# Weight loads on ScalarE's queue and set ask times in a planned DeltaNet and MLP kernel

## The chip, the cores and the metric

The kernel runs on one core of a Trainium2 chip. The metric is the device time of one execution in microseconds (us), as the median of several runs. Five engines work side by side on a core, each through its own instructions in order: TensorE (PE, matmuls), VectorE (DVE), ScalarE (ACT), GpSimd (POOL) and SyncE (SP, which here only issues DMA transfers). ACT and POOL can issue DMA transfers too. An engine that meets an instruction whose inputs are not ready stops there, and all that stands behind it waits.

## The reference

A delta-rule attention (4 batches, 8 heads, 768 tokens, head size 48), whose output goes through layer normalization and a two-layer MLP with a residual:

```python
for t in range(S):
    y[:, :, t] = np.einsum('bhd,bhde->bhe', q[:, :, t], state)
    v_old = np.einsum('bhde,bhd->bhe', state, kt)
    state = state + bt[:, :, :, None] * np.einsum('bhd,bhe->bhde', kt, vt - v_old)
...
xn = (x - mu) / np.sqrt(var + 1e-06) * g_ln
ch = np.maximum(xn @ w_ch1, 0.0) @ w_ch2
return (x + ch).astype(np.float32)
```

`kt` is the key divided by its norm. `x` is `y` with the heads side by side, 384 wide; `w_ch1` is 384 x 1536 and `w_ch2` 1536 x 384. All data is fp32.

## The kernel before

**Tiling.** The tokens are cut into 12 chunks of 64 (`C`), and a chunk is computed for all 32 sequences at once. Within a chunk the recurrence is solved in closed form: a triangular 64 x 64 system built from the products of keys (`gram`, tile `gsb`), whose inverse is `xt`. Chunk 0 gets its inverse by repeated matmuls (`first_inverse`, lines L853 to L910: products on PE, masks and transposes on DVE, copies into `xt` on ACT). Chunks 1, then 2 and 3, then 4 and 5 and so on get it by rows (`rows_inverse`): `gsb` is stored to DRAM (`gd`), loaded again with a sequence per partition (`gb`), ACT takes the norm (L1006), DVE works off one row after the other (L1025 and L1030), the result `xb` goes to DRAM (`xd`) and comes back as `xt`. `blocks_join` and `join` (PE at L1057, L1062, L1089, L1094) put the blocks of `xt` together. `recur` then makes u, the outputs y, the new state and the normalized `xnt` of the chunk, and `mlp` does the two products: the first at L1331 with a relu on ACT at L1340 into `h_all`; the second at L1353 for chunk 0, and for all others at L1429 in seven block products instead of eight. The first product of chunk 0 goes through two PSUM banks in turn.

**Weights.** They come in 12 pieces of 768 KB (`fetch`): six of `w_ch1`, then six of `w_ch2`, read as 32-bit words into five buffers. Pieces 0 and 1 go into `h_all`, the others in turn into three `words` buffers, so a piece from the sixth on can only be fetched when an earlier one is converted. Each is converted (`convert`) with two passes on ACT (L710, L718), one on DVE (L715) and one on POOL (L728), which writes `w_sb`.

**Other loads.** `load_raw` brings raw keys in four transfers of 96 KB (into `kr`, for chunk 3 into `tb`), `load_blocks` brings keys or queries in blocks of 32 tokens in eight small transfers (keys through POOL's queue, queries through SP's), `load_v` the values, and `norms` loads the diagonal of `gd` (`ksum`) with which the values are scaled. Almost all of it is issued by SP; ACT issues two loads of raw keys at the start.

**What sets the order.** The kernel does not issue as it goes. Every step is entered with `add` into a `Line`: its engine, an assumed cost, what it reads and writes, a priority (`pr`), for MLP products a due time (`due`), and an earliest time (`t0`). `Line.run` plays the whole kernel through on assumed times (`dma_go` moves the loads along, `LANES` = 8 loads on the way at most) and picks for each engine what comes next; `emit` issues the steps by planned start. `in_this_order` then ties each engine's instructions to that order. So `t0` and `due` are no waits on the chip: they move instructions within an engine's order. Where the plan leaves PE idle for long, `warm_up` puts in filler matmuls that compute nothing (L1507).

On the chip an instruction waits for semaphores. DMA transfers from SP and ACT share eight of them, and one that is issued waits until the eighth before it has landed.

Of the kernel before, what the change touches and what calls it, by code (L numbers as in the profile page):

```python
# [16 lines left out]
C = 64  # L17
# [6 lines left out]
@contextmanager  # L24
def in_this_order(tc):
    first = len(tc.nc.cur_bb.bb.instructions)
    last = {}
    yield last
    for ins in tc.nc.cur_bb.bb.instructions[first:]:
        if ins.engine not in ORDERED:  # L30
            continue
        if ins.engine in last:
            tc.add_manual_dep(
                ins, last[ins.engine].name,
                mybir.DependencyInfo(mybir.DependencyClass.NoSync, mybir.DependencyReason.DATA),
                reason="in_this_order",
            )
        last[ins.engine] = ins


PLAN = None
# [24 lines left out]
class Line:  # L66
# [6 lines left out]
    PE_TAIL, SWITCH = 0.12, 0.1  # L73
    BLOCK, FIRST, FETCH = 128, 93, 3.95
    WINDOW, WARM, KEEP = 3.413, 0.44, 0.6
    DMA_ISSUE, DMA_DONE, LANES = 1.35, 0.65, 8

    def __init__(self):
        self.steps = []
# [86 lines left out]
    def dma_go(self, until):  # L166

        while self.dma_t < until - 1e-12:
            on = [q for q in self.rings.values() if q and q[0][2] <= self.dma_t + 1e-12]
            lim = min([until] + [q[0][2] for q in self.rings.values() if q and q[0][2] > self.dma_t + 1e-12])  # L170
            if not on:
                self.dma_t = lim
                continue
            dt = min(lim - self.dma_t, len(on) * min(q[0][1] for q in on))
            for q in on:
                q[0][1] -= dt / len(on)
            self.dma_t += dt
            landed = False
            for q in on:
                if q[0][1] <= 1e-9:  # L180
                    s = q.pop(0)[0]
                    s.end = self.dma_t + self.DMA_DONE
                    self.done(s)
                    landed = True
            if landed:
                return True
        return False

    def dma_next(self):
        on = [q for q in self.rings.values() if q and q[0][2] <= self.dma_t + 1e-12]  # L190
        t = [q[0][2] for q in self.rings.values() if q and q[0][2] > self.dma_t + 1e-12]
        if on:
            t.append(self.dma_t + len(on) * min(q[0][1] for q in on))
        return min(t) if t else None

    def done(self, s):
# [191 lines left out]
def kernel(  # L388
# [28 lines left out]
    GH = 2 * H  # L417
# [11 lines left out]
    def sb(name, shape, dt=FP32):  # L429
# [12 lines left out]
    WORD_KEYS = [[("words", i)] for i in range(3)] + [  # L442
        [("h", 6 * i + f, g) for f in range(6) for g in range(2)] for i in range(2)
    ]
    tb = [sb(f"tb{i}", [128, GH * 64]) for i in range(3)]
    NKT, NQT, NPT, NG, NX, NV = 4, 2, 2, 4, 4, 2
# [31 lines left out]
    beta_b = sb("beta_b", [128, NSL, BK])  # L478
# [5 lines left out]
    ksum = [sb(f"ksum{i}", [128, GH]) for i in range(2)]  # L484
# [30 lines left out]
    def half(e):  # L515
        return slice(C * e, C * e + C)
# [15 lines left out]
    def dma(eng, out_, in_, n, ns, r=(), w=(), **kw):  # L532

        cost = 0.65 if eng != "SP" else 0.45 if n <= 512 else 0.62
        add(eng, cost, lambda: QUEUE[eng].dma_start(out=out_, in_=in_), r, w, bulk=n * ns / 16e3, **kw)  # L535
# [41 lines left out]
    for n in MASKED:  # L577
        k_, m, w = min(n, 4) if n == 6 else n, masks[n] if n < 6 else mask4, C if n < 6 else BK
# [52 lines left out]
    def load_padded(i, src, c, engs, **kw):  # L631
        for e in range(2):
            dma(
                engs[e], tb[i].rearrange("p (h d) -> p h d", d=DP)[half(e), :, 0:D], nat(src, c, e),
                GH * C, 16.5, [], [("tb", i, e, g) for g in range(2)], **kw,
            )

    def load_v(c, **kw):
        for e in range(2):
            dma("SP", vs[c % NV][half(e)], nat(v, c, e), GH * C, 16.5, w=[("v", c % NV, e)], **kw)  # L640

    def load_raw(c, engs=("SP", "SP"), dst=None, keys=None, **kw):

        dst = kraws[c % 3] if dst is None else dst
        for hp in range(2):
            for e in range(2):
                o = e ^ hp
                dma(
                    engs[e], dst.rearrange("p (h d) -> p h d", d=DP)[half(o), hp::2, 0:D],
                    k[2 * e : 2 * e + 2, hp::2, c * C : (c + 1) * C, :].rearrange("g h p d -> p (g h) d"),  # L650
                    NP * 2 * C, 16.5, [], [("kr", c % 3, o, hp)] if keys is None else [keys[2 * hp + e]], **kw,
                )

    def load_blocks(i, src, c, eng, **kw):
        dst = tb[i].rearrange("p (h u d) -> p h u d", u=2, d=BK)
        for hp in range(2):
            for m in range(2):
                w = min(BK, D - BK * m)
                p0 = DP * hp + BK * m
                for u in range(2):  # L660
                    t0 = c * C + BK * u
                    dma(
                        eng, dst[p0 : p0 + BK, :, u, 0:w],
                        src[:, hp::2, t0 : t0 + BK, BK * m : BK * m + w].rearrange("b j t d -> t (b j) d"),
                        GH * BK, 13.7 if w == BK else 11, [("tbpad", i)], [("tb", i, hp, m, u)],
                        after=[("tb", i, e, g, *o) for e in range(2) for g in range(2) for o in ((), (1,))], **kw,
                    )
# [25 lines left out]
    def fetch(i, **kw):  # L693
        dst = words[BUF[i]].rearrange("p n w -> p (n w)")
        src = pieces[i][1]
        if len(src.shape) == 3:
            dst = dst.rearrange("p (t n) -> p t n", t=2)
        dma("SP", dst, src, 256, 115, w=WORD_KEYS[BUF[i]], **kw)

    def convert(i, c0=0, n=WN, **kw):  # L700

# [410 lines left out]
    def norms(c, **kw):  # L1112
        i = c % 2
        flat = gpads[c % NG].rearrange("p h t -> (p h t)")
        w = GH * C
        for e in range(2):
            own = flat[e * C * w : e * C * w + C * (w + 1)].rearrange("(s x) -> s x", x=w + 1)[:, 0:w:C]
            dma("SP", ksum[i][half(e)], own, GH * C, 11, [("gd", c % NG)], [("ks", i, e)], **kw)
        kk = [("kn", i, n) for n in range(2)]
        add("ACT", 0.22, lambda: nc.scalar.sqrt(knrm[i], ksum[i]), [("ks", i, e) for e in range(2)], kk, **kw)  # L1120
        add("Pool", 0.2, lambda: nc.gpsimd.tensor_scalar_add(knrm[i], knrm[i], 1e-6), [], kk + [("kn", i)], **kw)
        scale_v(c, knrm[i], kk, **kw)
# [193 lines left out]
        return fbanks[turns[0] % 2] if not turns[1] else fbanks[turns[1] % 3]  # L1316

    def due(c, t):
        return 42.0 + 40.2 * c + 1.35 * t * (1.0 if c else 1.6) - (22.0 if c > 1 else 3.0 if c else 0.0)

    def mlp(c):
        xnt, x = xnts[c % 2], xs[c % 3]
# [176 lines left out]
        dma("Pool", brow[BK * e : BK * e + GH], beta[2 * e : 2 * e + 2, :, 0:C].rearrange("g h t -> (g h) t"), GH, 20, w=[("brow", e)], **chain)  # L1499
    load_v(0, pr=-79)  # L1500
    for i in range(3):
        fetch(i, pr=-70 + i)
    for i in range(3, 5):
        fetch(i, pr=-60 + i)

    def zeros():
        nc.tensor.matmul(f_[0][:, 256:512], nought, nought[:, 0:1].to_broadcast([128, 256]))  # L1507
# [26 lines left out]
    def prep_g(m):  # L1534
        pr = 20 * m - 15
        for c in (2 * m, 2 * m + 1):
            kt = (kts[c % NKT], ("kt", c % NKT))
            if c == 2:
                load_raw(c, pr=pr, t0=12.0)
                first_kt(kraws[2], raw_keys(2), *kt, PAIRS[3], pr=pr, t0=40.0)  # L1540
            elif c == 3:
                keys = [("tb", 2, e, hp) for hp in range(2) for e in range(2)]
                load_raw(c, dst=tb[2], keys=keys, pr=pr, t0=12.0)
                first_kt(tb[2], keys + [("tbpad", 2)], *kt, PAIRS[3], pr=pr, t0=40.0)
            else:
                load_blocks(2 * (c % 2), k, c, "Pool", pr=pr, t0=40.0 * m - 50)
                turned(c, 2 * (c % 2), *kt, pr=pr)
            gram(c, PAIRS[3 if m == 1 else 0], pr=pr, lag=0.5)

# [11 lines left out]
    for n, (p0, c, rows, cols) in enumerate(spots(BK, (0, 1))):  # L1561
        e, t0 = rows.start // C, c * C + cols.start
        dma(
            "SP", beta_b[p0 : p0 + GH],
            beta[2 * e : 2 * e + 2].rearrange("g h (m s) -> (g h) m s", m=NSL)[:, :, t0 : t0 + BK],
            96, 13.7, w=[("beta_b", n)], pr=5, t0=30.0,
        )

    def prep_x(m):
# [4 lines left out]

    def step(c):
        pr = 10 * c
        t0 = {2: 72.0, 3: 95.0}.get(c, 0.7)
        load_v(c, pr=pr - 5, t0=t0)
        if c > 2:
            load_raw(c, pr=pr - 5, t0=t0)  # L1580
        norms(c, pr=pr - 2)
        load_blocks(1, q, c, "SP", pr=pr - 3, t0=t0)
        turned(c, 1, qts[c % NQT], ("qt", c % NQT), pr=pr - 2)
        queries(c, pr=pr - 1, lag=0.5)
        recur(c, pr, lag=0.8)

    load_padded(1, q, 1, ("SP", "SP"), pr=8.2, t0=20.0)
    load_v(1, pr=8.1, t0=20.0)
    norms(1, pr=4)
    blocks_join(1, pr=3)  # L1590
    join(1, pr=3)
# [56 lines left out]
```

## Time and profile before

| what | value |
|---|---|
| median of 3 runs | 572.99 us (571.78 to 575.56) |
| profiled execution, its own time | 575.68 us |
| profiled execution, span from first to last instruction | 573.7 us |
| mean granted clock of TensorE | 0.964 |
| busy, PE / weight loads / DVE / ACT / POOL | 533.7 / 468.0 / 323.4 / 173.0 / 229.2 us |
| first MLP matmul of chunk 0 / of chunk 1 | 63.5 / 127.6 us |
| first product of the MLP, L1331 | 864 records, 209.8 us busy, 389 ns each |
| second product of chunks 1 to 11, L1429 | 924 records in three groups, 98.6 + 92.4 + 32.3 us busy |
| ten weight pieces into `words` | 768 KB each, median 10.0 us from issue to landing |
| two weight pieces into `h_all` | 768 KB each, median 6.4 us from issue to landing |
| moved by all DMA | 54.56 MB, 95 GB/s in the mean |

Times in the trace count from the start of the span. A matmul of the program is two records in the trace. Busy matmuls overlap, so busy time is more than what they cost one after the other. "SPq" is SP's queue of DMA issues, "ACTq" ACT's; a time beside them is that of issuing, not of the transfer. What stands in brackets with an arrow at a row of the timeline is the idle time of the engine before it, and what ended it. Idle time of an engine matters only where something waits for that engine.

### The profile page before, as it was taken

What the parts mean: (1) busy time and instruction counts of PE and PEld (TensorE: products, weight loads), DVE (VectorE), ACT (ScalarE), POOL (GpSimd) and SP (SyncE); (2) the same over time, 40 slices, a digit from 0 to 9 for tenths busy, and PEclk for the clock granted to TensorE, in tenths of its full rate; (3) what the DMA queues carried; (4) which work ended last, traced back from release to release, by engine and by line L of the source; (5) the groups of instructions that cost most, each with busy time, mean ns of one, the idle gap of its engine ahead of it and who ended that gap; (6) DMA issues with size and microseconds to landing.
All of it is one profiled execution on the core that took longest, in us unless ns stands there. A gap on an engine that the chain in (4) does not pass through costs nothing.

```text
span 573.7 us, 21608 instructions
## 1 busy us (share of the span) xinstructions
PE 533.7 (93%) x9482; PEld 468.0 (82%) x9482; DVE 323.4 (56%) x744; ACT 173.0 (30%) x403; POOL 229.2 (40%) x344
## 2 busy tenths in 40 slices
PE   8666977899899999999899998999999999999996
PEld 5555865668789898889789887889989899999996
DVE  5475858796699669973797634987423214010101
ACT  5676424342322412321322232212223122222120
POOL 4355747435337274454134231425232223424332
PEclk9788788999899999999799998999999999999999
DMA  9873569688556774667434476202510111110001
GB/s 160 264 134 65 135 158 178 162 171 147 59 85 115 207 102 89 129 149 142 62 86 85 121 143 100 64 16 58 129 32 2 56 31 42 27 29 15 8 22 27
DMA packets 195965, 54.56 MB, mean 95 GB/s; under 512 B 186136, under 2 KB 189344, under 8 KB 195872
## 3 DMA queue, kind: packets, MB, share of 16 engines
q1 hardware_dynamic: 192608, 49.83, 42.0%
q0 software_dynamic: 2208, 3.17, 3.5%
q8 instruction: 74, 1.21, 0.9%
q10 hardware_dynamic: 1056, 0.20, 0.2%
q14 instruction: 19, 0.16, 0.1%
HBM read 36.38 MB, written 16.78 MB: 93 GB/s over the span
## 4 chain that ended last, share of the span: by engine, by line
PE 66%; SPq 12%; DVE 9%; DMA 5%; issue 4%; ACT 2%; POOL 1%; ACTq 0%; DVEq 0%; POOLq 0%
PE f L1331 25%; PE f L1429 22%; SPq L535 12%; PE two L943 3%; DVE tmp L1025 2%; DVE xb L1030 2%; PE by L1198 2%; DMA words<-in_moe_w_ch_dram 2%; PE by L1136 2%; PE f L1094 2%; PE two L1191 2%; PE two L1208 1%; PE two L1136 1%; PE f L1089 1%; DMA gb<-gd 1%
## 5 line engine op out<-in xcount | busy, mean ns | idle before, releaser
L1331 PE MATMUL f<-xnt,w_sb 128*128 128x256 f32 x864 | 209.8, 389 | 2.4 <-ACT h_all L1340 2.0
L1331 PEld LDWEIGHTS f<-xnt,w_sb 128*128 128x128 f32 x864 | 164.1, 194 | 24.6 <-ACT h_all L1340 3.0
L1418 POOL TENSOR_TENSOR h_all<-h_all 128x256 f32<-128x256 f32 x99 | 73.3, 748 | 98.9 <-PE f L1429 56.4
L1340 ACT ACTIVATE h_all<-f 128x256 f32<-128x256 f32 x144 | 54.8, 383 | 174.9 <-PE f L1331 174.6
L1429 PE MATMUL f<-w_sb,h_all 128*128 128x192 f32 x396 | 98.6, 340 | 0.3 <-DVE rstd L1251 0.3
L1429 PE MATMUL f<-words,h_all 128*128 128x192 f32 x396 | 92.4, 333 | 0.0
L1454 POOL TENSOR_TENSOR words<-h_all 128x128 f32<-128x128 f32 x66 | 32.6, 495 | 123.5 <-ACT h_all L1340 114.1
L1429 PEld LDWEIGHTS f<-w_sb,h_all 128*128 128x128 f32 x396 | 70.8, 194 | 4.9 <-issue 0.6
L1030 DVE TENSOR_TENSOR xb<-xb,tmp 128x60 f32<-128x60 f32 (+19 forms) x170 | 69.8, 411 | 5.8
L1025 DVE TENSOR_TENSOR tmp<-xb,gb 128x60 f32<-128x60 f32 (+19 forms) x170 | 70.3, 413 | 4.9 <-POOL xb L1014 1.5
L1429 PEld LDWEIGHTS f<-words,h_all 128*128 128x128 f32 x396 | 69.5, 193 | 1.3 <-DVE o L1447 0.2
L1447 DVE TENSOR_TENSOR o<-f,x 128x192 f32<-128x192 f32 x33 | 11.6, 353 | 76.9 <-PE f L1429 76.0
L535 POOL DMA_DIRECT2D tb<-in_k_dram x64 | 42.4, 667 | 3.3 <-DVE tmp L1025 2.9
L1429 PE MATMUL f<-w_sb,words 128*128 128x192 f32 x132 | 32.3, 328 | 0.0
L1429 PEld LDWEIGHTS f<-w_sb,words 128*128 128x128 f32 x132 | 23.4, 190 | 0.5
L1236 ACT COPY x<-by 128x384 f32<-128x384 f32 x23 | 10.4, 480 | 43.8 <-POOL o L1447 25.9
L805 POOL TENSOR_TENSOR v<-v,knrm 128x768 f32<-128x768 f32 x11 | 16.7, 1515 | 16.3 <-DMA v<-in_v_dram 15.3
L728 POOL TENSOR_TENSOR w_sb<-words 128x768 uint32<-128x768 uint32 (+1 forms) x11 | 15.6, 1419 | 16.6 <-DVE words L715 11.0
L1082 DVE STREAM_TRANSPOSE xnj<-xt 128x512 f32<-128x512 f32 x11 | 7.7, 704 | 24.9 <-DMA xt<-xd 16.8
L1104 DVE COPY xt<-f 32x512 f32<-32x512 f32 x22 | 15.0, 682 | 10.5 <-PE f L1094 7.2
L1280 ACT ACTIVATE xnt<-xnt,g_sb 128x256 f32<-128x256 f32 x27 | 12.1, 499 | 28.6 <-DMA xnt<-xld 28.6
L1353 PE MATMUL f<-w_sb,h_all 128*128 128x384 f32 x48 | 17.9, 513 | 2.5 <-ACT h_all L1340 2.5
(205 smaller groups left out, 648.7 us busy)
## 6 DMA issues: line engine op xcount, KB each, us to landing
words<-in_moe_w_ch_dram SPq DMA_DIRECT2D x10, 768.0 KB, 10.0
gd<-gsb SPq DMA_DIRECT2D x11, 512.0 KB, 4.3
v<-in_v_dram SPq DMA_DIRECT2D x24, 192.0 KB, 4.3
out_dram<-o SPq DMA_DIRECT2D x48, 96.0 KB, 2.2
kr<-in_k_dram SPq DMA_DIRECT2D x46, 96.0 KB, 3.4
xld<-xlt SPq DMA_DIRECT2D x9, 384.0 KB, 2.9
xnt<-xld SPq DMA_DIRECT2D x36, 96.0 KB, 2.8
gb<-gd SPq DMA_DIRECT2D x40, 64.0 KB, 3.5
```

Of the source, the lines that this page charges most:

```text
L535: add(eng, cost, lambda: QUEUE[eng].dma_start(out=out_, in_=in_), r, w, bulk=n * ns / 16e3, **kw)
L805: lambda: nc.gpsimd.tensor_tensor(out=vs[c % NV], in0=vs[c % NV], in1=kn[:, :, None].to_broadcast([128, GH, D]), op=ALU.mult),
L943: nc.tensor.matmul(pair[hp][half(e ^ (hp & n)), (g * NP + j) * C : (g * NP + j + 1) * C], kt[drows(hp), l], rt[drows(hp), i],)
L1025: nc.vector.tensor_tensor(out=t, in0=xv[:, 0:n, j : j + 1].to_broadcast([128, n, w]), in1=gv[:, j : j + 1, j + 1 : L].to_broadcast([128, n ...
L1030: nc.vector.tensor_tensor(out=rest, in0=rest, in1=t, op=ALU.subtract)
L1136: nc.tensor.matmul(dst[half(e), hp, j], src[drows(hp), (e if n else key_half(c, hp, e)) * GP + j], s_all[drows(hp), e, j], start=(n == 0 o ...
L1331: nc.tensor.matmul(p[:, 0:TOK], w1_sb[:, t, f * 128 : (f + 1) * 128], xnt[:, t], start=(t == 0), stop=(t == KC - 1))
L1340: lambda hk=hk, p=p: nc.scalar.activation(h_all[:, hk] if c <= LNPE else h_all[:, hk].rearrange("p (g i b) -> p i g b", g=2, b=BK), p[:, 0 ...
L1353: lambda f=f, g=g, p=p, hk=hs[f]: nc.tensor.matmul(p[:, 0:DM], h_all[:, hk, g * 128 : (g + 1) * 128], w2_sb[:, f], start=(f == 0), stop=(f ...
L1418: add(eng, cost, lambda: e.tensor_tensor(out=out_, in0=x, in1=y, op=op), r, w, port=2 if eng == "Pool" else 1, pr=-2)
L1429: lambda f=f, t=start and f == 0: nc.tensor.matmul(p[:, 0:D2], lhs(f), rhs[:, f], start=t, stop=(f == F2 - 1), skip_group_check=True),
L1454: lambda f=f + i: e.tensor_tensor(out=s3[f], in0=one(0, 0)[0](f), in1=one(1, 0)[0](f), op=ALU.subtract),
```

## The change

Weight pieces are issued by ACT instead of SP. The first five get planned earliest times of 6, 10, 14, 18 and 22 us, where they had the default of 0.7. The raw keys of chunks 2 and 3 get 27 and 29 in place of 12, the key blocks of chunks 4 and 5 get 80 (30 before), of 6 and 7 120 (70), of later pairs 30 more than before; loads of `ksum`, `beta_b`, and of queries and values of chunks 1 to 3 get later times too. The planner's due times of the MLP are set anew, and it now assumes that loads take 1.4 times as long when four or more are under way. `in_this_order` also ties together loads that follow each other on different hardware queues. What is computed stays the same.

```diff
@@ in_this_order @@
+        if "DMA" in type(ins).__name__ and ins.engine != mybir.EngineType.Pool:
+            if queued is not None and queued.engine != ins.engine:
+                tc.add_manual_dep(
+                    ins, queued.name,
+                    mybir.DependencyInfo(mybir.DependencyClass.NoSync, mybir.DependencyReason.DATA),
+                    reason="in_this_order",
+                )
+            queued = ins
@@ class Line @@
-    DMA_ISSUE, DMA_DONE, LANES = 1.35, 0.65, 8
+    DMA_ISSUE, DMA_DONE, LANES, CROWD = 1.35, 0.65, 8, 1.4
@@ dma_go @@
-            dt = min(lim - self.dma_t, len(on) * min(q[0][1] for q in on))
+            share = len(on) * (1.0 if sum(len(q) for q in on) < 4 else self.CROWD)
+            dt = min(lim - self.dma_t, share * min(q[0][1] for q in on))
             for q in on:
-                q[0][1] -= dt / len(on)
+                q[0][1] -= dt / share
@@ fetch @@
-        dma("SP", dst, src, 256, 115, w=WORD_KEYS[BUF[i]], **kw)
+        dma("ACT", dst, src, 256, 115, w=WORD_KEYS[BUF[i]], **kw)
@@ norms @@
-            dma("SP", ksum[i][half(e)], own, GH * C, 11, [("gd", c % NG)], [("ks", i, e)], **kw)
+            dma(
+                "SP", ksum[i][half(e)], own, GH * C, 11, [("gd", c % NG)], [("ks", i, e)],
+                t0={1: 60.0, 2: 90.0, 3: 120.0}.get(c, 0.7), **kw,
+            )
@@ due @@
-        return 42.0 + 40.2 * c + 1.35 * t * (1.0 if c else 1.6) - (22.0 if c > 1 else 3.0 if c else 0.0)
+        return 47.0 + 41.0 * c + 1.35 * t * (1.0 if c else 1.63) - (31.4 if c > 1 else 16.9 if c else 0.0)
@@ the first five pieces @@
-        fetch(i, pr=-70 + i)
+        fetch(i, pr=-70 + i, t0=6.0 + 4 * i)
@@ prep_g @@
-                load_raw(c, pr=pr, t0=12.0)
+                load_raw(c, pr=pr, t0=27.0)
...
-                load_raw(c, dst=tb[2], keys=keys, pr=pr, t0=12.0)
+                load_raw(c, dst=tb[2], keys=keys, pr=pr, t0=29.0)
...
-                load_blocks(2 * (c % 2), k, c, "Pool", pr=pr, t0=40.0 * m - 50)
+                load_blocks(2 * (c % 2), k, c, "Pool", pr=pr, t0={2: 80.0, 3: 120.0}.get(m, 40.0 * m - 20))
@@ loads of beta_b, of chunk 1, and in step @@
-            96, 13.7, w=[("beta_b", n)], pr=5, t0=30.0,
+            96, 13.7, w=[("beta_b", n)], pr=5, t0=46.0,
...
-        t0 = {2: 72.0, 3: 95.0}.get(c, 0.7)
+        t0 = {2: 85.0, 3: 105.0}.get(c, 0.7)
...
-    load_padded(1, q, 1, ("SP", "SP"), pr=8.2, t0=20.0)
-    load_v(1, pr=8.1, t0=20.0)
+    load_padded(1, q, 1, ("SP", "SP"), pr=8.2, t0=42.0)
+    load_v(1, pr=8.1, t0=42.0)
```

In the built program the number of instructions is the same on every engine but for three things: twelve DMA issues leave SP (408 to 396 instructions) for ACT (407 to 419), and PE has 19 filler matmuls where it had 7. Line numbers in the changed file are 10 to 13 higher.

More of the change, by code (lines that the diff above doesn't have):

```diff
@@ L28, in in_this_order @@
     yield last
+    queued = None
     for ins in tc.nc.cur_bb.bb.instructions[first:]:
@@ L192, in dma_next @@
         if on:
-            t.append(self.dma_t + len(on) * min(q[0][1] for q in on))
+            t.append(self.dma_t + len(on) * (1.0 if sum(len(q) for q in on) < 4 else self.CROWD) * min(q[0][1] for q in on))
         return min(t) if t else None
@@ L1501 @@
     for i in range(3):
-        fetch(i, pr=-70 + i)
+        fetch(i, pr=-70 + i, t0=6.0 + 4 * i)
     for i in range(3, 5):
-        fetch(i, pr=-60 + i)
+        fetch(i, pr=-60 + i, t0=6.0 + 4 * i)
     def zeros():
```

## The prediction

> **What bounds the kernel now.** I read the busy shares in 40 slices first, to see where TensorE (PE) is not full. Each slice is 14.3 us.
>
> ```profile
> PE   8666977899899999999899998999999999999996
> DMA  9873569688556774667434476202510111110001
> ```
>
> PE is full from about slice 9 to the end. Only the first 130 us or so can be shortened; after that, time falls only if PE work is removed, and this change removes none. Next I cut the time between the first MLP matmul of chunk 0 (63.5 us) and that of chunk 1 (127.6 us) into stretches, and added one late stretch. Columns: stretch, its length, then busy us and instruction count for PE, weight load, DVE, ACT, POOL, then granted clock, DMA share and GB/s.
>
> ```profile
> 40.00:50.00 10.00, 7.11 (x187) 5.96 (x189) 4.06 (x11) 6.06 (x14) 5.42 (x8) 0.83 0.32 37
> ...
> 77.00:84.00 7.00, 4.08 (x136) 3.39 (x137) 5.12 (x16) 1.19 (x4) 4.11 (x7) 0.88 0.62 161
> 84.00:92.00 8.00, 4.68 (x139) 3.62 (x138) 6.31 (x15) 4.17 (x7) 5.73 (x8) 0.89 1.18 235
> 98.00:104.00 6.00, 4.18 (x101) 2.89 (x95) 1.13 (x4) 1.68 (x3) 1.62 (x1) 1.00 0.86 174
> ...
> 500.00:560.00 60.00, 60.00 (x322) 55.92 (x321) 4.29 (x12) 11.16 (x29) 22.98 (x39) 1.00 0.09 21
> ```
>
> PE idles 2.9 us at 40 to 50, then 2.9, 3.3 and 1.8 us in the three stretches of chunk 0's MLP; no engine is full there while DMA is. The chain of waits over the first 140 us names the cause: its summary, then its pieces (start, us, what).
>
> ```profile
> by line: SPq L535 27.9%; issue 9.7%; DMA words<-in_moe_w_ch_dram 7.3%; DVE xb L1030 4.3%; PE f L740 4.1%; PE f L1353 4.1%; DVE tmp L1025 3.7%; DMA v<-in_v_dram 2.9%; PE f L751 2.5%; DMA ksum<-gd 2.3%; PE f L943 2.2%; PE f L1331 1.7%; PE two
> ...
> 80.04 10.17 DMA words<-in_moe_w_ch_dram
> 90.30 0.90 ACT words L710
> 91.20 0.79 ACT words L718
> ...
> 92.39 1.45 PE f L1353 x2
> ```
>
> 39 us (27.9% of 140) is SP's queue issuing. Then the second MLP product waits for weights: asked for at 79.5 us, landed 10.2 us later, converted, used at 92.4. The timeline by engine shows why SP is late.
>
> ```profile
> 0.80 1.41 ACTq L535 DMA_DIRECT2D kr<-in_k_dram  x2
> 14.73 8.20 SPq L535 DMA_DIRECT2D kr<-in_k_dram  x2
> 19.29 0.36 PE L895 MATMUL two<-qt,gsb 64*64 64x64 f32 x1 [3.08 <-issue]
> 43.52 0.23 ACT L1006 ACTIVATE nrm_b<-gb 128x16 f32<-128x16 f32 x1 [2.62 <-DMA beta_b<-in_beta_dram]
> 44.85 2.08 PE L1507 MATMUL f<-u 128*128 128x256 f32 x4 [2.36 <-ACT xt L853]
> ...
> 82.84 9.74 SPq L535 DMA_DIRECT2D tb<-in_q_dram  x1
> ```
>
> Small loads issued behind five (14.73) or three (82.84) weight pieces hold SP for 8 to 10 us. Everything behind them (gd, gb, xd, ksum, the next pieces) slips. At 43.52 ACT waits for such a late gb load, its xt copies stand behind that wait, and PE waits for the copies.
>
> **The change, part by part.** In the built instruction order 12 weight fetches leave SP for ACT; the changed order also moves gd and seven of chunk 1's eight gb loads ahead of raw keys of chunks 2 and 3; the ksum loads of chunk 1 go behind its xt loads; 32 key-block issues on POOL (chunks 4 to 7) go behind weight conversions.
>
> Up to chunk 0's MLP (63.5 us). (a) gsb of chunk 1 was copied out by 17.4 us, but its gd store left at 27.5, behind the raw keys; with gd and gb now ahead of them, some 10 us earlier, ACT's norm is no longer late: PE's wait and the four filler matmuls that sit in it (2.36 + 2.08 us) mostly go, and the chunk 2 key transposes (L751, 1.8 us at 46.7) now stand earlier in PE's order, in a wait. Chunk 0's u products at 48.4 could start near 44.3: -4. (b) PE's "issue" waits at 16.2, 24.9 and 28.5 us sum to 3.08 + 1.19 + 1.47 = 5.7 us, at a DMA share of about 1. The Trainium skill ("Runtime: NRT & Kernel Launch", Instruction fetch mechanics) says fetching instructions has its own DMA queue and is mostly hidden; by that rule nothing comes back. The trace shows the waits, in the stretch where weights crowd the engines, but does not name the cause; bounds 0 and -5.7, I take -2. (c) ACT now issues five pieces here. By the two ACT issues of the trace 0.7 us each, 3.5 us on an engine that is 79% busy at 20 to 40 us and feeds PE: bounds 0 and +3.5, I take +2. Behind each issue stand qt and xt copies, for which PE waits. Sum: -4.
>
> Chunk 0's MLP (64.1 us). PE idles 9.2 us here, runs 2.0 us of filler (L1507 at 103.7), and starts cold (first 24 records of L1331 take 6.29 us, later 24 take 5.2). In the new order the six second-product pieces are asked for from before the MLP starts, each as soon as POOL has emptied its buffer, and SP can load xt for chunk 1 without weights ahead. DVE's chain of L1025/L1030 for chunk 1, which ended at 69.3, now stands complete before xnt of chunk 0. Conversions on POOL lose the key-block issues between them (16 x 0.65 = 10.4 us in 38 to 70 us, and 16 more in 79 to 98). All of it would give 9.2 + 2.0 + 1.1 = 12.3. I keep 3 us of waits, since ACT now issues the later pieces between the relus (L1340): -9. What moves out of this stretch (two gram products and one query product, 3 x 1.1 us) runs later and counts nothing.
>
> Here a rule speaks against the change. The Trainium skill ("DMA: Bandwidth & Descriptors", Issuing engines are not separate DMA queues) says that starting DMAs from several engines saves only the sequencer's issuing time, as all run on the same 16 DMA engines. By that, SP saves its twelve issues, 1.64 + 1.76 + 0.36 + 1.42 + 0.80 + 1.98 = 8.0 us, of which perhaps a quarter lies on the path: 571. The row says more: the issue of one small load took 9.74 us behind three pieces, against a median of 0.74 for such loads at 75 to 110 us. That is a hold, not issuing, and on ACT the pieces no longer stand before small loads. I go by the row.
>
> After 127.6 us. Nothing is removed. Twelve more filler matmuls (L1507) stand in PE's order, 19 for 7; one is two records of 0.25 us, so 0.5 us. Up to chunk 1's MLP they lie in waits for copies and cost nothing; if that cover is gone, 7 x 0.5 = +3.5. The last five (after chunk 1's and chunk 3's products) have no cover in the trace, which shows PE full there: +2.5. Key blocks of chunks 4 and 5 now start after 80 us: their grams stood at 118 to 123 and stand early in chunk 1's MLP now, with 16 issues (10.4 us) and a 3.5 us landing ahead; I see no delay. The later due times reorder PE but leave its work alone: 0, bounds -2 and +4.
>
> Sum: -4 - 9 + 2.5 = -10.5. The profiled execution took 575.7 us (span 573.7), 0.5% above the median of 573.0; the sum gives 565.2 for it, and 562.5 for the median.
>
> **The rivals.** (1) ACT takes over SP's hold, and the kernel is slower. ACT runs in order, and the fetches from the seventh piece on stand before relus; each waits for POOL's conversion of an earlier piece and, as all loads share eight semaphores, for the eighth load before it. The last piece waits for the landing of the one just before. PE has two banks for the first product, so about 2 x 1.3 us of cover. Two holds of 9.7 us cost 2 x (9.7 - 2.6) = 14, and the 9 us of the MLP stretch don't come: 573 - 4 + 2.5 + 14 = 586. It decides from about 8 us of hold beyond cover in all. For it: the 9.74 us row. Against: five pieces in a row (9.88 to 13.3 us) were issued at 0.7 us each without a hold, and ACT's row holds at most two or three. Chance 0.16.
>
> (2) Weights come in time, but the MLP stretch is then held by chunk 1's chain (xt, e, z, u, normalization) and by DVE, 98% busy at 110 to 130 us; fillers and ACT's issues use up the rest. Of the 9 us about 4 come, of the 4 one or two, less 2.5 to 3.5 of fillers: 570 to 574. For it: DVE's share. Against: DVE's share there is high because the chain of chunks 2 and 3, begun at 81 us, is late itself. Chance 0.18. That the change only relabels queues (the rule's 571) falls in here.
>
> **How the numbers follow.** The forecast case has 0.66, with its own range 554 to 568: down to -19 with all idle, filler and "issue" time gained, up to -5. The range reaches to 577, over rival (2) and the milder half of rival (1), and leaves out some 5% below 553 and 13% above. A measurement of this kernel can tell about 1% from no change, that is 567.3 and 578.7. Faster: 0.66, nearly all of the forecast case (0.64) and a little of rival (2). Within: 0.19. Slower: 0.15, rival (1) above 579.
>
> **What would show it.** Right: no small load on SP takes over 3 us to issue before 100 us; the first L1331 (L1344 in the changed file) starts near 59 us, that of chunk 1 near 110; no wait for words over 3 us; PE busy over 6.5 of 7 us in stretches of the MLP. Wrong: ACT's DMA issues last several us with relus behind them; PE waits for h_all copies; chunk 1's MLP starts after 122 us; or it starts early and PE shows new gaps after it, waiting for joins of chunks 2 and 3 or grams of 4 and 5.

## The result, and the profile after

The changed kernel takes 557.73 us (median of 4 runs, 552.84 to 559.73), the kernel before 572.66 us in the same session: a ratio of 0.972, with a 95% interval from 0.965 to 0.979. Ratios and intervals leave out executions more than 1.5% above the fastest of the same kernel; medians keep them. The profiled execution after took 552.84 us (span 551.1), the fastest of its four; the one before, 575.68 us, took longer than any of the four before. The two traces thus differ by 22.6 us of span where the medians differ by 15. Of the difference, 0.990 against 0.964 of mean granted clock is a part; it is weighed at the end.

First the 40 slices of the page after: busy share of PE, and that of the DMA engines.

```profile
PE   7567988999989999999999999999999999999996
DMA  9965993389565667258663457642131021100001
```

From slice 8 on PE is nearly full. Of the 8s that the row before had in its later part, at slices 11, 20 and 25, one is left, at slice 12. Next the same three stretches of both traces: up to chunk 0's first MLP product, from there to chunk 1's, and the rest. Columns: stretch, length, busy us and count for PE, weight load, DVE, ACT, POOL, then granted clock, DMA share, GB/s. Before:

```profile
0.00:63.53 63.53, 47.20 (x1290) 37.45 (x1291) 38.90 (x122) 40.74 (x95) 30.79 (x54) 0.85 0.72 152
63.53:127.61 64.08, 54.88 (x1099) 40.84 (x1095) 49.74 (x107) 23.82 (x44) 32.79 (x37) 0.93 0.76 167
127.61:573.70 446.09, 431.57 (x7099) 389.68 (x7097) 234.80 (x516) 108.47 (x264) 165.67 (x254) 0.98 0.39 77
```

And after:

```profile
0.00:58.17 58.17, 41.86 (x1242) 32.63 (x1243) 41.11 (x136) 40.85 (x94) 21.94 (x40) 0.97 0.78 185
58.17:112.21 54.04, 49.62 (x965) 35.89 (x963) 40.39 (x85) 20.46 (x42) 29.23 (x33) 0.97 0.64 131
112.21:551.10 438.89, 430.76 (x7300) 388.71 (x7300) 241.24 (x526) 111.41 (x269) 176.47 (x272) 1.00 0.43 84
```

The stretches are 5.4, 10.0 and 7.2 us shorter. Length less PE busy is PE's idle time: 16.3, 9.2 and 14.5 us before, 16.3, 4.4 and 8.1 after. So the first stretch gained without losing any idle time (its clock rose from 0.85 to 0.97, and some products moved behind the MLP's start), and the third, where nothing was expected, gave 7.2 us. Of the third's idle time 4.5 us stand behind the last matmul in both traces and could not go; the rest fell from 10.0 to 3.7 us.

The loads are asked for as the diff says. The chain of waits over the first 140 us has this summary now:

```profile
by line: PE f L1344 12.8%; issue 9.3%; DVE tmp L1035 8.5%; DVE xb L1040 8.4%; PE f L1442 3.8%; DMA words<-in_moe_w_ch_dram 3.5%; DMA kr<-in_k_dram 3.2%; PE two L953 3.1%; PE f L953 2.9%; PE f L1520 2.5%; DMA ksum<-gd 2.4%; PE f L920 2.2%; P
```

SP's queue, which led this list with 27.9%, is out of its first places; PE's own MLP products lead. The timeline of the changed kernel, some rows of SP's issues and two of PE (start, us, engine, line, operation; in brackets the idle time before):

```profile
6.78 5.39 SPq L545 DMA_DIRECT2D v<-in_v_dram  x2
21.58 5.25 SPq L545 DMA_DIRECT2D gb<-gd  x7
39.43 9.50 SPq L545 DMA_DIRECT2D beta_b<-in_beta_dram  x6
...
17.24 0.39 PE L905 MATMUL two<-qt,gsb 64*64 64x64 f32 x10 [1.38 <-issue]
24.48 0.79 PE L953 MATMUL f<-qt,kt 48*64 48x64 f32 x17 [3.60 <-issue]
```

gb is asked for from 21.6 us instead of 34.9. But small loads still take long to issue (5.39 us for two of v, the longer one 3.46), though not one weight piece stands on SP; and PE's "issue" waits are as long as they were.

### The profile page after: what moved, and what is told of

The parts are those of the page before. It is cut to its first block, busy times and chain, and to the rows that moved or that the text cites. A ratio compares the mean times of both kernels' runs of the same rounds, so it can differ in the third digit from the quotient of the medians.

```text
span 551.1 us, 21656 instructions
## 1 busy us (share of the span) xinstructions
PE 522.2 (95%) x9506; PEld 457.2 (83%) x9506; DVE 322.7 (59%) x744; ACT 172.7 (31%) x403; POOL 227.6 (41%) x344
## 4 chain that ended last, share of the span: by engine, by line
PE 79%; DVE 11%; issue 3%; DMA 2%; ACT 2%; POOL 1%; SPq 0%; ACTq 0%; DVEq 0%; POOLq 0%
PE f L1344 32%; PE f L1442 27%; PE two L953 4%; DVE xb L1040 3%; DVE tmp L1035 3%; PE two L1149 2%; PE f L1099 2%; PE f L1104 2%; PE two L1204 2%; PE by L1149 2%; PE by L1211 2%; PE f L1520 1%; PE two L1221 1%; DMA words<-in_moe_w_ch_dram 1%; DMA kr<-in_k_dram 1%
## 5 line engine op out<-in xcount | busy, mean ns | idle before, releaser
L1344 PE MATMUL f<-xnt,w_sb 128*128 128x256 f32 x864 | 204.8, 383 | 0.2 <-DVE st L1255 0.2
L1344 PEld LDWEIGHTS f<-xnt,w_sb 128*128 128x128 f32 x864 | 160.0, 190 | 21.0 <-ACT xnt L1315 0.4
L1442 PE MATMUL f<-w_sb,h_all 128*128 128x192 f32 x396 | 93.7, 331 | 0.0
L1442 PE MATMUL f<-words,h_all 128*128 128x192 f32 x396 | 90.6, 330 | 0.0
L1040 DVE TENSOR_TENSOR xb<-xb,tmp 128x60 f32<-128x60 f32 (+19 forms) x170 | 73.3, 431 | 5.8
L1442 PEld LDWEIGHTS f<-w_sb,h_all 128*128 128x128 f32 x396 | 69.1, 190 | 3.1 <-DVE o L1460 0.2
L1035 DVE TENSOR_TENSOR tmp<-xb,gb 128x60 f32<-128x60 f32 (+19 forms) x170 | 66.3, 390 | 3.3
L1460 DVE TENSOR_TENSOR o<-f,o 128x192 f32<-128x192 f32 x11 | 3.9, 351 | 28.0 <-PE f L1442 27.8
L1460 POOL TENSOR_TENSOR o<-o,words 128x192 f32<-128x192 f32 x22 | 13.1, 615 | 15.9 <-DVE words L1460 15.9
L1109 ACT ACTIVATE es<-f 32x512 f32<-32x512 f32 x22 | 13.0, 589 | 18.3 <-PE f L1099 15.6
```

The source lines that it names most:

```text
L1035: nc.vector.tensor_tensor(out=t, in0=xv[:, 0:n, j : j + 1].to_broadcast([128, n, w]), in1=gv[:, j : j + 1, j + 1 : L].to_broadcast([128, n ...
L1040: nc.vector.tensor_tensor(out=rest, in0=rest, in1=t, op=ALU.subtract)
L1344: nc.tensor.matmul(p[:, 0:TOK], w1_sb[:, t, f * 128 : (f + 1) * 128], xnt[:, t], start=(t == 0), stop=(t == KC - 1))
L1442: lambda f=f, t=start and f == 0: nc.tensor.matmul(p[:, 0:D2], lhs(f), rhs[:, f], start=t, stop=(f == F2 - 1), skip_group_check=True),
L1460: lambda: e.tensor_tensor(out=out_, in0=a, in1=b_, op=ALU.add), r, w, pr=pr,
```

## The experiments

The first question was the one that the prediction turned on: is it the queue that matters, or the order? Four kernels. In the first, the pieces go back to SP's queue at the very places where the plan has them:

```diff
-    def dma(eng, out_, in_, n, ns, r=(), w=(), **kw):
+    def dma(eng, out_, in_, n, ns, r=(), w=(), via=None, **kw):
...
-        add(eng, cost, lambda: QUEUE[eng].dma_start(out=out_, in_=in_), r, w, bulk=n * ns / 16e3, **kw)
+        add(eng, cost, lambda: QUEUE[via or eng].dma_start(out=out_, in_=in_), r, w, bulk=n * ns / 16e3, **kw)
...
-        dma("ACT", dst, src, 256, 115, w=WORD_KEYS[BUF[i]], **kw)
+        dma("ACT", dst, src, 256, 115, w=WORD_KEYS[BUF[i]], via="SP", **kw)
```

> The changed kernel with its plan kept: PE, DVE and POOL have the same instructions in the same order, and the twelve weight pieces are issued by SP at the places where the plan has them, instead of by ACT. Theory (small loads are held behind weight pieces on the same queue): issues of gb and raw keys on SP near 20 us and of xt or gb near 60 us take several us again, the first MLP product of chunk 0 starts at 61 us or later and that of chunk 1 at 118 or later, the time is 564 to 572. Rival (the new order alone brings the gain, the queue does not matter): 555 to 561, with the starts near 58 and 112 us. Rival (pieces on ACT cost ACT time): a little faster than the changed kernel, 553 to 556.

It takes 558.53 us, ratio 0.979 [0.972, 0.987]: the changed kernel's time within its spread. The queue itself is worth nothing that can be measured, though the two MLP starts, 60.2 and 115.6 us, lie 2 to 4 us behind those named. With a piece ahead of them on their own queue, the two loads of v that take 5.39 us to issue in the changed kernel take 1.50 us here. The second is the reverse, the plan of before with its pieces issued by ACT (`via="ACT"` at the fetch, and the new ties in `in_this_order`).

> The kernel before with its plan kept, and only the twelve weight pieces issued by ACT at the places where the plan has them. Theory of the hold: the raw keys of chunks 2 and 3 and the query blocks at 83 us issue in under 2 us each, chunk 0's MLP starts near 61 and chunk 1's near 121, time 562 to 568. Rival (order alone): 570 to 574. Rival (ACT held instead): ACT's issues take several us and the time is over 575.

It takes 583.1 us, ratio 1.022 [1.010, 1.033], slower than before. Rows of its timeline, SP's issues and ACT's (start, us, queue):

```profile
6.69 9.78 SPq L544 DMA_DIRECT2D v<-in_v_dram  x2
19.84 6.48 SPq L544 DMA_DIRECT2D kr<-in_k_dram  x4
...
8.25 0.96 ACTq L544 DMA_DIRECT2D words<-in_moe_w_ch_dram  x2
76.69 1.49 ACTq L544 DMA_DIRECT2D words<-in_moe_w_ch_dram  x3
```

Two loads of v hold SP for 9.78 us (the longer one 8.20) while the weights run from ACT's queue, whose own issues take 0.33 to 0.44 us. So a load need not stand behind a piece on the same queue to be held. Nor is it the wait for the eighth load before: the semaphore that the held load of v needs had been free since 5.6 us, when the last load that used it landed. What is left is that many large transfers were under way, which was not tested by itself. And the three pieces at 76.7 us, which stood behind chunk 1's `xt` loads while both were SP's, now run beside them. The time from issue to landing of these eight `xt` loads, before and in a2:

```profile
DMA to landing us min/median/max: 1.8/2.0/2.3
DMA to landing us min/median/max: 1.9/2.4/11.9
```

DVE can make `xnj` only when all of `xt` is there, and PE pays (the table of waits: engine, line, releaser, total, times, longest):

```profile
PE f L1066 <- DVE xnj L1060: 10.2, 1, 10.2
```

The third kernel is the changed one with the old `due`:

```diff
-        return 47.0 + 41.0 * c + 1.35 * t * (1.0 if c else 1.63) - (31.4 if c > 1 else 16.9 if c else 0.0)
+        return 42.0 + 40.2 * c + 1.35 * t * (1.0 if c else 1.6) - (22.0 if c > 1 else 3.0 if c else 0.0)
```

> The changed kernel with the old due times of the MLP. Theory (the due times only reorder PE's work, which is full anyway): 555 to 561, stretch from chunk 1's first MLP product to the end within 3 us of the changed kernel's 438.9 us. Rival (the later half gained because PE's order changed with the due times): 563 to 568, with more waits of PE after 112 us.

554.93 us, ratio 0.974 [0.966, 0.981]: the due times are not the source. The fourth takes the filler matmuls out and leaves the order as it is; they compute nothing that is used.

```diff
-        nc.tensor.matmul(f_[0][:, 256:512], nought, nought[:, 0:1].to_broadcast([128, 256]))
+        pass
```

> The changed kernel without its 19 filler matmuls; all other instructions stand as they were. They compute nothing that is used. Theory of the forecast (fillers in the first 112 us lie in waits, the last five have no cover): 1 to 3 us faster than the changed kernel, 554 to 557. Rival (fillers keep PE's clock up in the waits): 1 to 6 us slower, with granted clock under 0.9 in stretches of the first 60 us where the changed kernel has 0.91 to 1.00.

559.38 us, ratio 0.981 [0.974, 0.989], 1.6 us above the changed kernel, with intervals that overlap: the fillers cost nothing that can be measured. The stretch up to chunk 0's MLP in this kernel:

```profile
0.00:57.78 57.78, 42.81 (x1221) 33.94 (x1221) 40.64 (x135) 41.07 (x93) 21.98 (x39) 0.88 0.75 177
```

The granted clock is 0.88 where it was 0.97 with them; in one execution of each.

The order it was, then. Which of the new numbers makes the order? Four more kernels put the new start times (`t0`) to the test. First, the changed kernel with all of them back:

```diff
-                t0={1: 60.0, 2: 90.0, 3: 120.0}.get(c, 0.7), **kw,
+                **kw,
...
-        fetch(i, pr=-70 + i, t0=6.0 + 4 * i)
+        fetch(i, pr=-70 + i)
...
-                load_raw(c, pr=pr, t0=27.0)
+                load_raw(c, pr=pr, t0=12.0)
...
-                load_blocks(2 * (c % 2), k, c, "Pool", pr=pr, t0={2: 80.0, 3: 120.0}.get(m, 40.0 * m - 20))
+                load_blocks(2 * (c % 2), k, c, "Pool", pr=pr, t0=40.0 * m - 50)
...
```

> The changed kernel with every planned start time put back (weight pieces unspaced; raw keys of chunks 2 and 3 from 12 us; key blocks from 40m-50; ksum, q, v and beta as before). What stays of the change: the pieces on ACT's queue, the crowding factor in the planner, the new due times. Theory A (the set later times make the gain: small loads ahead of weights, POOL free for the weight conversions): the time goes back to 570 to 580, the MLP stretch of chunk 0 to 62 to 66 us. Rival B (the crowding factor and the due times make it, through the order that the planner then finds): 556 to 562, the stretch at most 58 us.

570.7 us, ratio 0.997 [0.992, 1.002]: the whole gain is gone, as theory A has it, but its stretch of chunk 0's MLP, 74.9 us in the profiled execution, is longer than A gave it. Next, only the spacing of the first pieces and the raw keys of chunks 2 and 3 go back (the second and third of the edits above):

> The changed kernel with the first five weight pieces unspaced and the raw keys of chunks 2 and 3 asked for from 12 us again; all other times as changed, POOL's conversions still ahead of its key-block loads. Theory A1 (what counts is that gd, gb and the small loads stand ahead of raw keys and weights before chunk 0's MLP): first MLP product at 62 to 64 us in place of 58, whole 562 to 566. Rival A2 (POOL's order counts): within 3 us of the changed kernel, 555 to 561.

575.4 us, ratio 1.008 [1.004, 1.012], far above what either theory gave it. Then the key blocks alone (the last edit above):

> The changed kernel with the key-block start times alone put back (40m-50: 30 us for chunks 4 and 5, 70 for 6 and 7), so that POOL issues block loads of chunks 4 and 5 between its weight conversions again. Theory A2 (the MLP stretch of chunk 0 was shortened because POOL's conversions no longer stand behind block loads): the stretch goes from 54 to 60 to 64 us, whole 564 to 570. Rival A1 (the loads before chunk 0's MLP count): within 3 us of the changed kernel, 555 to 561, stretch 53 to 57 us.

569.1 us, ratio 0.999 [0.995, 1.003]. The time is the one of A2, but its stretch of chunk 0's MLP was 55.3 us, the one of A1: right time, wrong place. And the new key-block times put into the kernel before:

> The kernel before with the new key-block start times alone (80 us for chunks 4 and 5, 120 for 6 and 7, 40m-20 after), pieces on SP's queue, nothing else changed. Theory A2 (block loads out of the way of conversions and weights make the gain in chunk 0's MLP): stretch 64 to 55 to 58 us, whole 562 to 567. Rival A1: within 3 us of the kernel before, 569 to 575, stretch 61 to 66 us.

582.4 us, ratio 1.017 [1.006, 1.028], slower, which neither expected (its profiled execution, at 574.9 us, is the fastest of its four, so its trace does not show why). The stages of these kernels do not break where the theories looked. In b2, chunk 0's MLP starts at 61.0 and chunk 1's at 115.8 us, only some 3 us later than in the changed kernel; the loss lies behind. Its three stretches up to chunk 1's MLP, up to chunk 2's normalized `xnt` (the transposes at L1299, which stand ahead of its MLP), and after; columns as above:

```profile
0.00:115.75 115.75, 99.41 (x2276) 75.04 (x2276) 66.85 (x199) 62.60 (x136) 49.87 (x72) 0.96 0.71 157
115.75:180.80 65.05, 56.05 (x958) 48.02 (x957) 53.06 (x108) 11.57 (x29) 31.10 (x49) 0.90 0.61 97
180.80:573.20 392.40, 383.27 (x6312) 346.78 (x6306) 198.08 (x439) 98.51 (x239) 144.15 (x223) 1.00 0.38 77
```

And the filler matmuls alone in the second of them (PE busy, weight load, clock, DMA):

```profile
115.75:180.80 65.05, 10.64 (x33) 6.90 (x32) 0.90 0.61 97
```

Chunk 2 comes at 180.8 us instead of 160.2. In the wait for it PE idles 9.0 us and runs 10.6 us of fillers: a hole that the plan saw coming and filled. The row-by-row inverse on DVE for chunks 2 and 3, on which chunk 2 hangs, ends with these rows, in b2 and in the changed kernel:

```profile
143.74 0.21 DVE L1040 TENSOR_TENSOR xb<-xb,tmp 128x31 f32<-128x31 f32 x1
118.76 0.22 DVE L1040 TENSOR_TENSOR xb<-xb,tmp 128x31 f32<-128x31 f32 x1
```

In b3 it ends at 140.8 us. From that end to chunk 2's `xnt` it is 35 to 45 us in all the kernels here (36.0 before, 41.2 after, 36.9 in b2, 36.5 in b3). DVE had time: over 60 to 100 us it was busy for 14.4 us in b2 and 28.2 in the changed kernel. So start times moved for a few loads re-plan everything behind them, and what was measured is the new plan more than the loads.

Chunk 2's start thus cuts the kernel in two. From there to the end it was 409 us before and 391 after, and b2 and b3 have 392 and 391 as well, b4 411. What divides them is how much of chunk 1's MLP is done by then, and b1 to b3 share with the changed kernel three things: ACT's queue, the due times and the planner's crowding factor. The last four kernels take these apart. The changed kernel with the factor at 1:

```diff
-    DMA_ISSUE, DMA_DONE, LANES, CROWD = 1.35, 0.65, 8, 1.4
+    DMA_ISSUE, DMA_DONE, LANES, CROWD = 1.35, 0.65, 8, 1.0
```

> The changed kernel with the planner's crowding factor at 1.0 in place of 1.4; everything else, start times, ACT's queue and due times, as changed. Theory P (the factor is what lets the plan place DMA waits truly, and so brings the weights early): by chunk 2's start at most 230 of the MLP products are done in place of 276, and the whole is 566 to 576. Rival Q (the later start times and ACT's queue do it, the factor is small): 276 products, chunk 2's start 160 to 166, whole 553 to 563.

569.75 us, ratio 0.997 [0.993, 1.001]. All the gain is gone with this one number, though the first stretches are as short as in the changed kernel (chunk 0's MLP from 58.7 us, chunk 1's from 113.1). The expectations of these four count the records of all MLP products that PE has done by chunk 2's start, at most 276. Of these, 192 are done by then in every kernel; the other 84 are chunk 1's second product. So I count that one, of which the rows below show what ran before chunk 2's `xnt` and what ran after, all later chunks' included. Columns: stretch, length, PE busy and count, weight load, clock, DMA. In c1:

```profile
0.00:157.60 157.60, 3.55 (x16) 2.75 (x16) 0.89 0.76 154
157.60:566.00 408.40, 167.70 (x908) 150.95 (x908) 0.99 0.37 74
```

In the changed kernel:

```profile
0.00:160.20 160.20, 15.04 (x84) 13.57 (x84) 0.98 0.74 151
160.20:551.10 390.90, 153.06 (x840) 138.37 (x840) 0.99 0.38 78
```

With the factor PE has finished the 84 when chunk 2 comes; without it 16 are done and 68 are left. At 153.06 / 840 = 0.182 us each these are 12.4 us, more than c1's lead of 2.6. The clock differs in the first row, 0.89 and 0.98, and not in the second: it can move when chunk 2 comes, and not what is left from there. The other part is in PE's waits from the start of chunk 1's MLP to the end, in c1 all but the first of them behind chunk 2's start. In c1:

```profile
PE f L1104 <- issue: 2.3, 1, 2.3
PE by L1149 <- issue: 2.3, 2, 1.5
PE f L1344 <- DVE o L1460: 2.2, 1, 2.2
PE f L1104 <- ACT es L1109: 1.5, 1, 1.5
PE f L1344 <- ACT h_all L1353: 1.0, 1, 1.0
PE f L1442 <- ACT words L1473: 0.9, 1, 0.9
```

In the changed kernel there are four left, and one of a size:

```profile
PE by L1299 <- DVE xln L1267: 2.1, 1, 2.1
PE f L1520 <- ACT u L1206: 0.9, 1, 0.9
PE two L953 <- DVE s_all L1231: 0.3, 1, 0.3
PE f L1344 <- DVE st L1255: 0.2, 1, 0.2
```

The next kernel is the changed one with the pieces planned on SP as well as issued there (`dma("SP", ...)` in `fetch`), in whatever order the planner then finds.

> The changed kernel with the weight pieces planned on and issued by SP, in the order that the planner then finds; start times, crowding factor and due times as changed. Theory R (planning the pieces on a queue of their own is what lets them be asked for between 40 and 76 us): the last piece is asked for after 95 us, 210 to 240 products by chunk 2's start, whole 566 to 576. Rival Q (the start times do it, whichever queue): last piece before 85 us, 276 products, whole 555 to 563.

552.76 us, ratio 0.973 [0.963, 0.982], all 84 records done, the last piece asked for at 76.2 us. ACT's queue is not needed in the plan either, nor are the ties between queues. Then the kernel before with nothing but the new start times:

> The kernel before with all of the new start times (pieces spaced, raw keys at 27 and 29, key blocks, ksum, q, v, beta) and nothing else: SP's queue, no crowding factor, the old due times. Rival Q (the start times alone make the gain, through the earlier first inverse and the earlier weights): first inverse's store before 60 us, last piece before 85 us, whole 555 to 563. Theory P or R (queue or factor needed): 566 to 578.

568.56 us, ratio 0.996 [0.991, 1.001]. They do on the chip what they should: chunk 0's MLP starts at 51.9 us, the earliest of all, the last piece is asked for at 73.3 us, and the inverse for chunks 2 and 3 ends at 115.1. The time moves by 0.4%, not clear of no change, and 38 of the 84 are done by chunk 2's start. Last, the kernel before with the factor alone (and the ties, which there bind only the two loads that ACT issues at the start):

> The kernel before with the planner's crowding factor alone (1.4): SP's queue, old start times, old due times. Theory P (the factor is sufficient for the early weights): 260 to 276 products by chunk 2's start, whole 558 to 566. Rivals Q and R: 210 to 230 products, whole 568 to 580.

560.81 us, ratio 0.985 [0.976, 0.994]: 84 done, 388.5 us left from chunk 2's start, which comes late, at 168.6 us. All in one table. The start of chunk 2 and the time from there are those of the profiled execution, which lies within 3.1 us of the kernel's median but for b1 (5.9 us above), c2 (4.3 above), b4 (7.5 below) and the changed kernel (4.9 below):

| kernel | factor | median us | ratio | of 84 done | chunk 2 at | from there |
|---|---|---|---|---|---|---|
| before | 1 | 572.7 | 1 | 26 | 164.4 | 409.3 |
| changed | 1.4 | 557.7 | 0.972 | 84 | 160.2 | 390.9 |
| a1 same plan, SP | 1.4 | 558.5 | 0.979 | 84 | 163.8 | 392.9 |
| a2 old plan, ACT | 1 | 583.1 | 1.022 | 26 | 171.6 | 409.4 |
| a3 old due | 1.4 | 554.9 | 0.974 | 72 | 162.5 | 391.3 |
| a4 no fillers | 1.4 | 559.4 | 0.981 | 84 | 164.9 | 392.5 |
| b1 old start times | 1.4 | 570.7 | 0.997 | 84 | 185.1 | 389.5 |
| b2 early asks | 1.4 | 575.4 | 1.008 | 84 | 180.8 | 392.4 |
| b3 old key blocks | 1.4 | 569.1 | 0.999 | 84 | 177.3 | 390.8 |
| b4 before, new key blocks | 1 | 582.4 | 1.017 | 18 | 162.2 | 410.6 |
| c1 factor 1 | 1 | 569.8 | 0.997 | 16 | 157.6 | 408.4 |
| c2 SP, planned anew | 1.4 | 552.8 | 0.973 | 84 | 162.4 | 393.0 |
| c3 before, new start times | 1 | 568.6 | 0.996 | 38 | 160.3 | 408.1 |
| c4 before, factor 1.4 | 1.4 | 560.8 | 0.985 | 84 | 168.6 | 388.5 |

The last column has two values, 389 to 393 with the factor and 408 to 411 without, whatever else is changed, and from chunk 2's start the clock is 0.99 or 1.00 in every one. The factor buys some 18 us after chunk 2's start; the start times decide when chunk 2 comes. With the factor, start times that are only partly new bring chunk 2 at 177 to 181 us and lose all of it. What the full set of new start and due times adds over the old one shows in c2 against c4, whose ratios' intervals overlap but which ran in one session: all four executions of c2 (551.6 to 557.1 us) are faster than all four of c4 (558.9 to 562.2), by 8 us in the medians. But b1 against c4 (old start times in both, but ACT's queue and new due times in b1) shows that the old start times go well with one setting of the rest and badly with another. No version beat the changed kernel clearly: a3 and c2 have its ratio.

## Why the prediction was right, and where it was not

The forecast of 562.5 us (553 to 577) holds the 557.7, 4.8 us too high, and the case that it gave most of the chance came. Its reasons fared worse than its number: one of them is refuted, most of the gain hangs on a part of the change that the sum has no term for, and that the total came near is in part luck.

**"That is a hold, not issuing, and on ACT the pieces no longer stand before small loads. I go by the row."** This step failed. The row was real, its reading wrong: a1 has the pieces on SP and the changed kernel's time, a2 has them on ACT and SP is still held, 9.78 us for two loads. The trace before could have warned: the first two loads behind the five pieces took 1.32 us to issue and the third was held, and between the three pieces and the 9.74 us two loads of `ksum` took 1.73 us. The rule that I set aside was right: the Trainium skill ("DMA: Bandwidth & Descriptors", Issuing engines are not separate DMA queues) says that all issuers run on the same 16 DMA engines. It would have put the change of queue at about nothing, as measured; its 571, though, left out the order.

**No term for the crowding factor.** The sum goes through what moves where on each engine and calls the order's later part "0, bounds -2 and +4" and the rest +2.5. Measured, the rest gave -7.2 us. The step behind it, "Only the first 130 us or so can be shortened", failed too: 10.0 us of idle time sat in fourteen waits of PE between 127 us and its last matmul, none over 2.2 us and so none that drops a slice below 8, and 3.7 remain. c1 shows the term that was missing: without the factor the kernel takes 569.75 us, and c4 gives it from the other side, 12.4 us gained by the factor alone.

**Up to chunk 0's MLP, -4:** -5.4 measured, for other reasons. (a) ACT's norm came 6.5 us earlier (37.03 after 43.52), as forecast, but PE's idle time in the stretch stayed at 16.3 us. (b) -2 for the "issue" waits did not come: 1.38 + 3.60 + 0.34 = 5.3 us in the first 30 us, 5.7 before. By the rule weighed there nothing comes back, and nothing did; what these waits are, no run here shows. (c) ACT's issues of pieces took 0.33 to 0.68 us each, all but one at most 0.40, in place of 0.7.

**Chunk 0's MLP, -9:** -10.0, with 4.4 us of idle left where 3 were kept. The size is right and the earlier weights are in the trace (last piece at 75.6 us, 109.3 before at the latest). But c1 has this stretch at 54.4 us, as short as the changed kernel, and is no faster at the end: what was gained here was lost behind chunk 2's start. A stage's length alone was no measure of the gain. (The piece that landed 10.2 us after its issue was the second of three, asked for at 80.04 us and not at 79.5; nothing hangs on it.)

**Fillers, +2.5:** a4 puts them at -1.6, within the spread. Due times at 0: right, by a3.

**The rivals.** ACT's holds (586) did not come in the changed kernel. But a2, at 583, is the slower side that it stood for, by another way: weights that run beside `xt` loads instead of behind them. The second rival's stretch "held by chunk 1's chain and by DVE" did not come in the changed kernel; b2 and b3 show its like one chunk later, and 569 to 575 us.

**Of the marks to look for,** chunk 0's MLP at 58.2 and chunk 1's at 112.2 us were near the 59 and 110 named; PE busy over 6.5 of 7 us was missed in three of six stretches between 67 and 109 us (5.38 to 6.03); one wait for words took 3.8 us; and a v load of 3.46 us breaks "no small load on SP over 3 us".

**What stays open.** How the factor leads the planner to put chunk 1's MLP ahead of chunk 2's work was read from the orders and not isolated further; an argued way, not shown, is that loads which the plan lets land later no longer draw the work that waits for them forward on PE. No factor but 1.0 and 1.4 was tried. And part of the gain may be clock: over 51 runs of the kernel before in three sessions, 0.01 of granted clock goes with 2.6 us, and the medians of clock, 0.967 there and 0.983 in the changed kernel, would make 4 of the 15 us. If all of PE's busy time went with the clock, they would make 8.5 (an estimate: 533.7 us x 0.016). In the two profiled executions PE is busy for 533.7 and 522.2 us, so that 11.5 of their 22.6 us lie there, and the rest in idle time. The clock is not chance of one session: a1, with the same plan in another, had 0.972 to 0.982 where the kernel before had 0.963 to 0.973. Whether fewer waits raise the clock, these runs don't tell.

## What to carry to other kernels

Where an order is planned offline, test each constant of the plan by itself and in both directions: here one factor in the model of crowded loads carried most of the gain, and start times that looked like the point were worth nothing measurable without it and some 8 us with it. Judge such a change at a point where the work done can be counted (84 records, or 16), by that count and by when the point comes, and not by the length of one stage: b1 to b3 have all 84 done and gain nothing, since chunk 2 comes 17 to 25 us later. And before a long issue is put down to the queue it stands in, look at what else the DMA engines carry at that time.

## What was not expected of the hardware

- A small load's issue can be held about as long when the weights are on another engine's queue: 8.20 us for one load of v with the five pieces on ACT, beside the 9.74 us before behind pieces on its own queue, and against about 0.6 us for loads of v later. The semaphore that it needed was free.
- Three pieces that ran beside eight small `xt` loads, instead of behind them on one queue, put off the longest of these from 2.3 to 11.9 us between issue and landing, and cost PE one wait of 10.2 us.
- Taking 19 filler matmuls out went with a granted clock of 0.88 instead of 0.97 in the first 58 us, in one execution each, and with 1.6 us in the medians.
